# The first row tiles of a fused attention and FFN kernel: two PSUM tiles for the transposes, another load order, an earlier Sqrt table

## Chip, cores, metric

One core of a Trainium2 chip. The time is the device time of one execution in microseconds (us), median of several runs called fast (granted TensorE clock 0.998 to 1.000). The "span" is the time from the first to the last instruction of one profiled execution, about 1.8 us shorter than the device time of the same run.

Terms: a weight *piece* is one transfer; it has *landed* when the last of the 16 DMA engines that share it is through. A *PSUM tile* is a buffer for TensorE's results. A *hole* is a pause of TensorE between two matmuls. A *late run* is one that lies more than 0.5 us above the median of its kernel.

## The reference

`x` is (1, 2048, 640) in bf16. Cut to what matters:

```python
xn = (x - mean(x)) / sqrt(var(x) + 1e-5)            # per row of 640
s = attention(xn @ wq, k_cache[-512:], v_cache[-512:]) @ wo
g = silu((silu(xn @ w_gate) * (xn @ w_up)) @ w_down)  # hidden 1536
out = x + s * g
```

Everything starts with the normalisation and the FFN. This study is about the first 16 us of 924: the first rows of `x` and the first quarter of `w_gate` and `w_up` come in, four tiles of 128 rows are normalised, transposed on TensorE and multiplied by the first three hidden groups (f = 0 to 2, a gate and an up product each, so six PSUM banks). From group 3 on, matmuls of 512 columns run on all four row tiles at once.

## The kernel before

The loads. SyncE and ScalarE share them; the Sqrt table comes behind all of ScalarE's:

```python
load_x(0)                       # rows 0-63 on SyncE, 64-127 on ScalarE
load_x(1, nc.scalar)
for cs in (slice(0, 1), slice(1, 3), slice(3, NC)):     # NC = 5 chunks of 128 rows
    if cs.stop == NC:
        load_x(2)
    for eng, w_sb, w in ((nc.sync, wg_sb, B_w_gate), (nc.scalar, wu_sb, B_w_up)):
        ...                     # chunks cs, first 384 columns
load_x(3)
load_gu(1)                      # next quarter of both matrices
...
nc.scalar.activation(act_t[:], one_t[:], ACT.Sqrt)      # loads the table
keep_warm(11)                   # zero matmuls, 512 columns
```

The row tiles. All five transposes go into one PSUM tile, one or two copies take them out:

```python
def ready(t):
    ln_transpose(t)             # five TensorE transposes into tps[t], part of one tile tp
    n = NC if t else 2
    nc.scalar.copy(xnT[:, 0:n, rows], tps[t][:, 0:n, :])
    if n < NC:
        nc.vector.tensor_copy(out=xnT[:, n:NC, rows], in_=tps[t][:, n:NC, :])
...
ready(0); ln_sqrt(1); keep_warm(3)
for t in range(4):
    order = [(*fs, [c]) for c in range(NC) for fs in banks]      # chunk by chunk
    if t:
        order = [(*fs, range(NC)) for fs in banks]               # bank by bank
    for k, (f, s, cs) in enumerate(order):
        if k == len(order) * 3 // 5 and t < 3:
            ...                 # normalise tile t+1, ready(t + 1), statistics of the next
        hidden_mm(first[f][s][:, rows], s, f, rows, cs)
```

Then the loop over the hidden groups:

```python
for f in range(NF):
    if b or f >= 3:
        ffn_hidden(b, f)        # matmuls, Silu on ScalarE, product hT on VectorE
    if nx and 1 <= f < 5:
        ln_stats(4 * b + 3 + f) # statistics of the next block's row tiles, on VectorE
    if nx and 5 <= f < 9:
        ...                     # their normalisation and DMA transposes
```

The softmax here doesn't subtract the row's maximum and nothing guards it: scores larger than these inputs give would overflow.

Of the kernel before, what the change touches and what calls it, by code (L numbers as in the profile page):

```python
# [9 lines left out]
ACT = mybir.ActivationFunctionType  # L10
# [5 lines left out]
def kernel(  # L16
# [13 lines left out]
    nc = tc.nc  # L30
    P = nc.NUM_PARTITIONS

    x2 = A_x.flatten_outer_dims()
# [9 lines left out]
    NC = D // P  # L43
# [10 lines left out]
    bf = dt.bfloat16  # L54
    f32 = dt.float32
# [10 lines left out]
    wpool = ctx.enter_context(tc.tile_pool(name="att_w", bufs=2))  # L66
    kpool = ctx.enter_context(tc.tile_pool(name="att_k", bufs=1))
    qpool = ctx.enter_context(tc.tile_pool(name="att_q", bufs=2))
    psum = ctx.enter_context(tc.tile_pool(name="psum", bufs=2, space=bass.MemoryType.PSUM))

    def sc_tile():
        return psum.tile([P, 2, 512], f32, name="sc", tag="sc")

    def mm_tile():
        return psum.tile([P, 2, 512], f32, name="mm", tag="mm")


    ctx.enter_context(tc.manual_schedule())
# [1 line left out]
    xnT = res.tile([P, NC, Sq], bf, name="xnT")  # L80
# [3 lines left out]
    ident = consts.tile([P, P], bf, name="ident")  # L84
# [3 lines left out]
    one_t = consts.tile([P, 1], f32, name="one_t")  # L88
    nc.vector.memset(one_t[:], 1.0)
    act_t = consts.tile([P, 1], f32, name="act_t")  # L90
# [52 lines left out]
    def sum_k(pr, c):  # L143
        d = pairs[pr]
        nc.vector.reduce_sum(d["ssum"][:, c : c + 1], d["KT"][:, c, :], axis=AX.X)

    lo, hi = slice(0, 64), slice(64, 128)
# [17 lines left out]
    with ExitStack() as fctx:  # L165
# [6 lines left out]
        zero_t = ffw.tile([P, 512], bf, name="zero_t")  # L172
        nc.vector.memset(zero_t[:], 0.0)
        wg_sb = ffw.tile([P, NC, F], bf, name="wg_sb")
        wu_sb = ffw.tile([P, NC, F], bf, name="wu_sb")
        wd_sb = ffw.tile([P, NF, D], bf, name="wd_sb")
        FQ = F // 4
        x_t, ln, xns = {}, {}, {}

        def load_x(t, eng=nc.sync):  # L180
            x_t[t] = lnx.tile([P, D], bf, name="x_t")
            if t == 0:
                for r, eng in ((lo, nc.sync), (hi, nc.scalar)):
                    eng.dma_start(out=x_t[t][r, :], in_=x2[t * P + r.start : t * P + r.stop, :])
            else:
                eng.dma_start(out=x_t[t][:], in_=x2[t * P : (t + 1) * P, :])

        def load_gu(q):
            cols = slice(q * FQ, (q + 1) * FQ)
# [4 lines left out]
                out=wu_sb[:, :, cols], in_=B_w_up[:, cols].rearrange("(c p) f -> p c f", p=P)  # L194
            )

        load_x(0)
        load_x(1, nc.scalar)
        for cs in (slice(0, 1), slice(1, 3), slice(3, NC)):
            if cs.stop == NC:  # L200
                load_x(2)
            for eng, w_sb, w in ((nc.sync, wg_sb, B_w_gate), (nc.scalar, wu_sb, B_w_up)):
                src = w[cs.start * P : cs.stop * P, 0:FQ].rearrange("(c p) f -> p c f", p=P)
                eng.dma_start(out=w_sb[:, cs, 0:FQ], in_=src)
        load_x(3)
        load_gu(1)
        for t in range(4, 8):
# [3 lines left out]
        nc.sync.dma_start(out=wd_sb[:], in_=B_w_down.rearrange("(f p) d -> p f d", p=P))  # L211


        nc.scalar.activation(act_t[:], one_t[:], ACT.Sqrt)
        warm = sc_tile()

        def keep_warm(n):
            for _ in range(n):
                nc.tensor.matmul(warm[:, 0, :], zero_t[:, 0:P], zero_t[:], start=True, stop=True)

        keep_warm(11)

        def ln_stats(t, between=None):
            b, ti = divmod(t, 4)
            if ti == 0:
                ln[b] = [lnw.tile([P, 4, 2], f32, name="mv"), lnw.tile([P, 4], f32, name="rstd")]
            stats = lnw.tile([P, ng, nc.vector.BN_STATS_DIM], f32, name="stats")
            for g in range(ng):
                nc.vector.bn_stats(stats[:, g, :], x_t[t][:, g * (D // ng) : (g + 1) * (D // ng)])
                if g == 0 and between:  # L230
                    between()
            nc.vector.bn_aggr(ln[b][0][:, ti, :], stats[:])
# [7 lines left out]
        def ln_sqrt(t):  # L240
            mv, rstd = ln[0]
            nc.scalar.activation(
                rstd[:, t : t + 1], mv[:, t, 1:2], ACT.Sqrt, bias=eps_t[:], scale=1.0
            )
# [10 lines left out]
                    op0=ALU.subtract, op1=ALU.mult,  # L255
                )

        tps = {}

        def ln_transpose(t):  # L260
            xn = xns.pop(t)
            tps[t] = tp[:, t % 2, 0 : NC * P].rearrange("p (c k) -> p c k", c=NC)
            for c in range(NC):
                nc.tensor.transpose(tps[t][:, c, :], xn[:, c * P : (c + 1) * P], ident[:])

        def ln_transpose_dma(t):
            nc.sync.dma_start_transpose(
                out=xnT[:, 0:NC, t * P : (t + 1) * P], in_=xns.pop(t)[:]
            )
# [3 lines left out]
        def hidden_mm(out, s, f, qc, cs=range(NC)):  # L273
            w_sb = (wg_sb, wu_sb)[s]
            for c in cs:
                nc.tensor.matmul(  # L276
                    out, w_sb[:, c, f * P : (f + 1) * P], xnT[:, c, qc],
                    start=(c == 0), stop=(c == NC - 1),
                )

        def hidden_gate(b, f, g, u):
            sg = ffa.tile([P, 512], bf, name="sg")
            nc.scalar.activation(sg[:], g, ACT.Silu)  # L283
            nc.vector.tensor_tensor(hTs[b][:, f, :], u, sg[:], ALU.mult)  # L284

        def ffn_hidden(b, f):
            gu = mm_tile() if (b, f) == (0, 3) else sc_tile()
            for s in range(2):
                hidden_mm(gu[:, s, :], s, f, slice(b * 512, (b + 1) * 512))
            hidden_gate(b, f, gu[:, 0, :], gu[:, 1, :])  # L290

        def ffn_down(b, u):
            ti, n = divmod(u, 2)
# [23 lines left out]
        hTs[0] = ffh.tile([P, NF, 512], bf, name="hT")  # L317


        first = {f: [sc[:, s, :] for s in range(2)] for f, sc in ((0, sc_tile()), (1, sc_tile()))}  # L320
        tp = psum.tile([P, 2, 1024], bf, name="tp", tag="mm")
        first[2] = [mm[:, s, :] for mm in (mm_tile(),) for s in range(2)]
        def ready(t):
            ln_transpose(t)
            rows = slice(t * P, (t + 1) * P)
            n = NC if t else 2
            nc.scalar.copy(xnT[:, 0:n, rows], tps[t][:, 0:n, :])
            if n < NC:
                nc.vector.tensor_copy(out=xnT[:, n:NC, rows], in_=tps[t][:, n:NC, :])

        ln_stats(0)
        ln_sqrt(0)
        ln_stats(1, lambda: ln_apply(0, (slice(0, 2 * P), slice(2 * P, D))))
        ready(0)
        ln_sqrt(1)
        keep_warm(3)
        banks = [(f, s) for f in range(3) for s in range(2)]
        for t in range(4):
            rows = slice(t * P, (t + 1) * P)

            order = [(*fs, [c]) for c in range(NC) for fs in banks]
            if t:
                order = [(*fs, range(NC)) for fs in banks]
            for k, (f, s, cs) in enumerate(order):
                if k == len(order) * 3 // 5 and t < 3:
                    if t == 1:
                        ln_stats(3, lambda: ln_apply(2))
                    else:
                        ln_apply(t + 1)
                    ready(t + 1)  # L350
                    if t == 0:
                        ln_stats(2)
                    if t < 2:
                        ln_sqrt(t + 2)
                    else:
                        nc.scalar.activation(act_t[:], one_t[:], ACT.Silu)
                hidden_mm(first[f][s][:, rows], s, f, rows, cs)
                if t == 3 and s == 1:
                    hidden_gate(0, f, *first[f])
        nc.gpsimd.memset(V_p[:, :, :, Dh : Dh + 2], 1.0)  # L360

        for b in range(NB):
            if b:
                hTs[b] = ffh.tile([P, NF, 512], bf, name="hT")
            nx = b + 1 < NB
            u = 0
            for f in range(NF):
                if nx and b and f == 0:
                    for t in range(4 * b + 4, 4 * b + 8):
                        load_x(t)  # L370
                if b or f >= 3:
                    ffn_hidden(b, f)
                if nx and 1 <= f < 5:
                    ln_stats(4 * b + 3 + f)
                    if f == 4:
                        ln_rstd(b + 1, 0, 4)
                if nx and 5 <= f < 9:
                    ln_apply(4 * b + f - 1)
                    ln_transpose_dma(4 * b + f - 1)

                if b >= 1 and f % 3:
                    ffn_down(b - 1, u)
                    u += 1
                if b == 2:
                    if f == 0:
                        load_k(0)
                    elif 2 <= f < 6:
                        transpose_k(0, f - 2)
                    elif f == 6:
                        load_wq(0)  # L390
                    elif 7 <= f < 10:
                        sum_k(0, f - 7)
                elif b == 3:
                    if f < 5:
                        centre_k(0, f)
                    elif f < 8:
                        (load_k, load_wq, load_wo)[f - 5]((1, 1, 0)[f - 5])
# [360 lines left out]
```

## Time and profile before

| | before |
|---|---|
| device time, first three runs | 925.28 us (924.81 to 925.31) |
| span of the profiled run | 923.7 us |
| first real matmul | 6.91 us |
| first 512-column matmul (group 3) | 15.83 us |

TensorE sets the time, and after 15.83 us it waits for nothing that counts; so that start is the number to watch. The lines are shown in the prediction. A timeline line reads: start us, duration us, engine, source line, operation, `out<-in`, shapes, count; in brackets the idle time before it and what ended that. Several equal instructions in a row are merged, and matmuls overlap: one of 128 columns is shown 0.22 us long while the next starts 0.055 us after it. The distance of the starts is what a matmul costs.

### The profile page before, as it was taken

The page shows a single profiled execution, that of the slowest core. Times are in us where ns is not written, and L with a number is a line of the kernel's source. Part 1 is how long each engine was busy: PE and PEld are TensorE (multiplying, and loading weights), DVE is VectorE, ACT ScalarE, POOL GpSimd, SP SyncE. Part 2 cuts the span into 40 slices and gives each one's busy share as a digit, 9 for nine tenths or more (in the row PEclk, how much of TensorE's full clock was granted, in tenths as well). Part 3 has the DMA queues.
Part 4 walks back from the last instruction along what each step waited for, and adds up shares of the span by engine and source line. Part 5 has one row for each costly group of instructions (what it writes and reads, how often), then busy time and mean ns, then how long its engine had stood idle before and what let it go on. Part 6 is the DMA issues. An engine that isn't in the chain of part 4 may idle for free.

```text
span 923.7 us, 25785 instructions
## 1 busy us (share of the span) xinstructions
PE 917.0 (99%) x11101; PEld 626.2 (68%) x11101; DVE 576.2 (62%) x844; ACT 473.7 (51%) x847; POOL 100.1 (11%) x387
## 2 busy tenths in 40 slices
PE   9999999999999999999999999999999999999997
PEld 5455555575858585868686867676767777776665
DVE  6433331467676767676666667676767676767655
ACT  4222223546464656555556565655555555556561
POOL 0000000000000000000000000000000000002977
PEclk9999999999999999999999999999999999999999
DMA  9321510035544434444536252636271717162524
GB/s 294 77 53 35 114 35 1 1 71 95 83 82 83 83 79 87 74 91 68 98 59 106 60 107 53 112 51 115 44 121 41 126 37 129 36 132 74 135 57 140
DMA packets 243810, 77.18 MB, mean 84 GB/s; under 512 B 224624, under 2 KB 243696, under 8 KB 243696
## 3 DMA queue, kind: packets, MB, share of 16 engines
q1 hardware_dynamic: 242640, 74.72, 41.5%
q8 instruction: 87, 1.43, 0.7%
q10 hardware_dynamic: 1056, 0.82, 0.3%
q14 instruction: 27, 0.22, 0.1%
HBM read 39.45 MB, written 2.62 MB: 46 GB/s over the span
## 4 chain that ended last, share of the span: by engine, by line
PE 98%; DMA 1%; DVE 0%; ACTq 0%; issue 0%; DVEq 0%
PE mm L430 22%; PE sc L565 19%; PE sc L444 18%; PE mm L470 16%; PE sc L276 11%; PE mm L298 6%; PE sc L539 3%; PE mm L522 2%; PE mm L539 1%; DMA wu_sb<-in_B_w_up_dram 1%; PE mm L276 0%; PE mm L311 0%; PE sc L522 0%; PE sc L470 0%; PE mm L444 0%
## 5 line engine op out<-in xcount | busy, mean ns | idle before, releaser
L448 ACT ACTIVATE p_t<-sc 128x1024 bf16<-128x1024 f32 x254 | 252.9, 1022 | 128.6 <-PE sc L444 128.6
L435 DVE TENSOR_REDUCE qT<-mm 128x512 bf16<-128x1024 f32 x189 | 231.0, 1223 | 92.5 <-PE mm L430 90.0
L500 ACT ACTIVATE O_b<-mm,r 128x192 bf16<-128x192 f32 x486 | 164.6, 421 | 183.4 <-issue 159.2
L430 PE MATMUL mm<-xnT,wq_p 64*128 64x512 bf16 x1890 | 240.2, 377 | 0.0
L590 DVE TENSOR_TENSOR sacc<-sacc,sc 128x640 f32<-128x640 f32 x200 | 164.3, 821 | 89.5 <-PE sc L565 89.5
L565 PE MATMUL sc<-wo_p,OT_b 64*128 64x320 bf16 x2592 | 217.4, 296 | 0.0
L444 PE MATMUL sc<-qT,khat 64*128 64x512 bf16 x1524 | 198.4, 377 | 0.1
L470 PE MATMUL mm<-V_p,p_t 64*128 64x193 bf16 x3520 | 186.5, 243 | 0.0
L470 PEld LDWEIGHTS <-p_t 64*128 64x128 bf16 x3584 | 162.9, 93 | 12.3 <-issue 0.4
L430 PEld LDWEIGHTS <-wq_p 64*128 64x128 bf16 x1890 | 105.7, 94 | 94.5 <-issue 0.5
L565 PEld LDWEIGHTS <-OT_b 64*128 64x128 bf16 x2592 | 140.7, 94 | 21.1
L444 PEld LDWEIGHTS <-khat 64*128 64x128 bf16 x1536 | 85.9, 94 | 79.0 <-issue 0.4
L553 POOL MEMSET turn_t<- 128x1 f32 x328 | 32.2, 98 | 696.4 <-PE mm L470 474.0
L284 DVE TENSOR_TENSOR hT<-sc,sg 128x512 bf16<-128x512 f32 x46 | 31.7, 690 | 85.2 <-ACT sg L283 85.1
L283 ACT ACTIVATE sg<-sc 128x512 bf16<-128x512 f32 x46 | 27.3, 596 | 72.4 <-PE sc L276 72.4
L276 PE MATMUL sc<-xnT,wu_sb 128*128 128x512 bf16 (+1 forms) x260 | 59.1, 355 | 0.5 <-DMA wu_sb<-in_B_w_up_dram 0.5
L276 PE MATMUL sc<-xnT,wg_sb 128*128 128x512 bf16 (+1 forms) x260 | 59.2, 355 | 0.0
L298 PE MATMUL mm<-wd_sb,hT 128*128 128x320 bf16 x384 | 56.6, 300 | 0.0
L489 DVE RECIPROCAL r<-mm 128x4 f32<-128x4 f32 x124 | 22.6, 183 | 47.4 <-PE mm L470 35.9
L298 PEld LDWEIGHTS <-hT 128*128 128x128 bf16 x384 | 37.5, 98 | 18.9
L276 PEld LDWEIGHTS <-wu_sb 128*128 128x128 bf16 x285 | 26.3, 98 | 27.4 <-DMA wu_sb<-in_B_w_up_dram 0.7
L276 PEld LDWEIGHTS <-wg_sb 128*128 128x128 bf16 x285 | 26.4, 98 | 23.1
(68 smaller groups left out, 373.6 us busy)
## 6 DMA issues: line engine op xcount, KB each, us to landing
wo_p<-in_A_wo_dram SPq DMA_DIRECT2D x16, 480.0 KB, 4.3
K_p<-in_A_k_cache_dram SPq DMA_DIRECT2D x32, 192.0 KB, 3.1
V_p<-in_A_v_cache_dram SPq DMA_DIRECT2D x32, 192.0 KB, 3.0
wq_p<-in_A_wq_dram SPq DMA_DIRECT2D x64, 80.0 KB, 3.2
wq_p<-in_A_wq_dram SPq DMA_DIRECT2D x16, 160.0 KB, 3.5
x_r<-in_A_x_dram SPq DMA_DIRECT2D x16, 160.0 KB, 3.7
x_t<-in_A_x_dram SPq DMA_DIRECT2D x14, 160.0 KB, 3.1
OT_b<-O_b SPq DMA_TRANSPOSE x124, 2.8
```

Source lines behind the costliest of these rows:

```text
L276: nc.tensor.matmul(out, w_sb[:, c, f * P : (f + 1) * P], xnT[:, c, qc], start=(c == 0), stop=(c == NC - 1),)
L298: nc.tensor.matmul(dn[:, 0:HD], hTs[b][:, f, ti * P : (ti + 1) * P], wd_sb[:, f, cols], start=(f == 0), stop=(f == NF - 1),)
L430: nc.tensor.matmul(q_ps[:, h, :], pairs[pr]["wq"][r, c, j * P : (j + 1) * P], xnT[r, c, b * 512 : (b + 1) * 512], start=(c == 0), stop=(c ...
L435: nc.vector.reduce_sum(qTs[i][:, j, :], q_ps[:, :, :].rearrange("p h n -> p n h"), axis=AX.X)
L444: nc.tensor.matmul(sc[:, h, :], khat[r, j, ks], qT[r, j, :], start=(j == 0), stop=(j == 2))
L448: nc.scalar.activation(p_t[:, :, :], sc[:, :, :], ACT.Exp, scale=scale)
L470: m = nc.tensor.matmul(acc[:, k, h * 256 : h * 256 + Dh + 1], Ps[i][kc][r, h, qt * P : (qt + 1) * P], V_p[r, kc, h, 0 : Dh + 1], start=(p ...
L500: nc.scalar.activation(O_b[:, qt, h, :], a_k[:, h, 0:Dh], ACT.Copy, scale=r[:, k, h, :])
L539: nc.tensor.matmul(ps, OTs[i][:, 3 * qt + j, :], pairs[i // NB]["wo"][:, j, n * HD : (n + 1) * HD], start=(first and j == 0), stop=(end an ...
L553: st["turn"] = nc.gpsimd.memset(turn_t[:], 0.0)
L565: m = nc.tensor.matmul(ps[:, n, 0:HD], OTs[i][r, 3 * qt + j, :], pairs[i // NB]["wo"][r, j, n * HD : (n + 1) * HD], start=(turn == 0 and j ...
L590: nc.vector.tensor_tensor(s_t, s_t, sc[:, :, 0:HD], ALU.add)
```

## The change

Its intent: bring the first weights in earlier (one queue, four large pieces, x tiles 0 and 1 on the other queue), start the first matmuls after two transposes rather than five, and have the Sqrt table ready. The core of the diff:

```diff
-        load_x(0)
+        load_x(0, nc.scalar)
         load_x(1, nc.scalar)
-        for cs in (slice(0, 1), slice(1, 3), slice(3, NC)):
-            ...  (gate pieces on SyncE, up pieces on ScalarE, x tile 2 between)
+        load_first(slice(0, 2))          # gate and up, both on SyncE
+        load_first(slice(2, NC))
+        nc.scalar.activation(act_t[:], one_t[:], ACT.Sqrt)
+        load_x(2)
         load_x(3)
...
-        keep_warm(11)
+        keep_warm(9)
+        keep_warm(6, P)
...
         def ready(t):
-            ln_transpose(t)
-            ...
+            for tp, cs in zip(tps, PARTS):       # PARTS = chunks 0-1, chunks 2-4
+                for k, c in enumerate(range(cs.start, cs.stop)):
+                    nc.tensor.transpose(tp[:, k, :], xn[:, c * P : (c + 1) * P], ident[:])
+            ...  (one copy for each part; both on ScalarE, the second on VectorE for t == 3)
-        keep_warm(3)
...
-            if t:
+            if t == 3:
                 order = [(*fs, range(NC)) for fs in banks]
-                if k == len(order) * 3 // 5 and t < 3:
+                if k == len(order) * 4 // 5 and t < 3:
...
+        ffn_hidden(0, 3, [...])                  # group 3, in the banks of the two transpose tiles
+        early.close()                            # then the early PSUM pool gives way to "mm"
...
-                if b or f >= 3:
+                if b or f >= 4:
                     ffn_hidden(b, f)
```

Group 3 has to leave the loop, as it uses the early PSUM pool.

More of the change, by code (lines that the diff above doesn't have):

```diff
@@ L68 @@
     qpool = ctx.enter_context(tc.tile_pool(name="att_q", bufs=2))
-    psum = ctx.enter_context(tc.tile_pool(name="psum", bufs=2, space=bass.MemoryType.PSUM))
+    sc_pool = ctx.enter_context(tc.tile_pool(name="psum_sc", bufs=2, space=bass.MemoryType.PSUM))
+    mm_pool = []
     def sc_tile():
-        return psum.tile([P, 2, 512], f32, name="sc", tag="sc")
+        return sc_pool.tile([P, 2, 512], f32, name="sc")
     def mm_tile():
-        return psum.tile([P, 2, 512], f32, name="mm", tag="mm")
+        return mm_pool[0].tile([P, 2, 512], f32, name="mm")
     ctx.enter_context(tc.manual_schedule())
@@ L181, in load_x, with load_first @@
             x_t[t] = lnx.tile([P, D], bf, name="x_t")
-            if t == 0:
-                for r, eng in ((lo, nc.sync), (hi, nc.scalar)):
-                    eng.dma_start(out=x_t[t][r, :], in_=x2[t * P + r.start : t * P + r.stop, :])
-            else:
-                eng.dma_start(out=x_t[t][:], in_=x2[t * P : (t + 1) * P, :])
+            eng.dma_start(out=x_t[t][:], in_=x2[t * P : (t + 1) * P, :])
+        def load_first(cs):
+            for w_sb, w in ((wg_sb, B_w_gate), (wu_sb, B_w_up)):
+                src = w[cs.start * P : cs.stop * P, 0:FQ].rearrange("(c p) f -> p c f", p=P)
+                nc.sync.dma_start(out=w_sb[:, cs, 0:FQ], in_=src)
         def load_gu(q):
@@ L195, in load_gu @@
             )
-        load_x(0)
+        load_x(0, nc.scalar)
         load_x(1, nc.scalar)
-        for cs in (slice(0, 1), slice(1, 3), slice(3, NC)):
-            if cs.stop == NC:
-                load_x(2)
-            for eng, w_sb, w in ((nc.sync, wg_sb, B_w_gate), (nc.scalar, wu_sb, B_w_up)):
-                src = w[cs.start * P : cs.stop * P, 0:FQ].rearrange("(c p) f -> p c f", p=P)
-                eng.dma_start(out=w_sb[:, cs, 0:FQ], in_=src)
+        load_first(slice(0, 2))
+        load_first(slice(2, NC))
+        nc.scalar.activation(act_t[:], one_t[:], ACT.Sqrt)
+        load_x(2)
         load_x(3)
@@ L211, with keep_warm @@
         nc.sync.dma_start(out=wd_sb[:], in_=B_w_down.rearrange("(f p) d -> p f d", p=P))
-        nc.scalar.activation(act_t[:], one_t[:], ACT.Sqrt)
-        warm = sc_tile()
-        def keep_warm(n):
-            for _ in range(n):
-                nc.tensor.matmul(warm[:, 0, :], zero_t[:, 0:P], zero_t[:], start=True, stop=True)
-        keep_warm(11)
+        early = ExitStack()
+        psum1 = early.enter_context(tc.tile_pool(name="psum1", bufs=1, space=bass.MemoryType.PSUM))
+        PARTS = (slice(0, 2), slice(2, NC))
+        tps = [psum1.tile([P, 8, P], bf, name="tp", tag="tp%d" % n) for n in range(2)]
+        first = [
+            [gu[:, s, :] for s in range(2)]
+            for gu in (sc_tile(), sc_tile(), psum1.tile([P, 2, 512], f32, name="gu"))
+        ]
+        def keep_warm(n, cols=512):
+            for _ in range(n):
+                nc.tensor.matmul(
+                    first[2][1][:, 0:cols], zero_t[:, 0:P], zero_t[:, 0:cols], start=True, stop=True
+                )
+        keep_warm(9)
+        keep_warm(6, P)
         def ln_stats(t, between=None):
@@ L256, in ln_apply @@
                 )
-        tps = {}
-        def ln_transpose(t):
-            xn = xns.pop(t)
-            tps[t] = tp[:, t % 2, 0 : NC * P].rearrange("p (c k) -> p c k", c=NC)
-            for c in range(NC):
-                nc.tensor.transpose(tps[t][:, c, :], xn[:, c * P : (c + 1) * P], ident[:])
         def ln_transpose_dma(t):
@@ L284, in hidden_gate, with ffn_hidden @@
             nc.vector.tensor_tensor(hTs[b][:, f, :], u, sg[:], ALU.mult)
-        def ffn_hidden(b, f):
-            gu = mm_tile() if (b, f) == (0, 3) else sc_tile()
+        def ffn_hidden(b, f, gu=None):
+            gu = gu or [sc[:, s, :] for sc in (sc_tile(),) for s in range(2)]
             for s in range(2):
-                hidden_mm(gu[:, s, :], s, f, slice(b * 512, (b + 1) * 512))
-            hidden_gate(b, f, gu[:, 0, :], gu[:, 1, :])
+                hidden_mm(gu[s], s, f, slice(b * 512, (b + 1) * 512))
+            hidden_gate(b, f, *gu)
         def ffn_down(b, u):
@@ L317 @@
         hTs[0] = ffh.tile([P, NF, 512], bf, name="hT")
-        first = {f: [sc[:, s, :] for s in range(2)] for f, sc in ((0, sc_tile()), (1, sc_tile()))}
-        tp = psum.tile([P, 2, 1024], bf, name="tp", tag="mm")
-        first[2] = [mm[:, s, :] for mm in (mm_tile(),) for s in range(2)]
         def ready(t):
-            ln_transpose(t)
-            rows = slice(t * P, (t + 1) * P)
-            n = NC if t else 2
-            nc.scalar.copy(xnT[:, 0:n, rows], tps[t][:, 0:n, :])
-            if n < NC:
-                nc.vector.tensor_copy(out=xnT[:, n:NC, rows], in_=tps[t][:, n:NC, :])
+            xn, rows = xns.pop(t), slice(t * P, (t + 1) * P)
+            for tp, cs in zip(tps, PARTS):
+                for k, c in enumerate(range(cs.start, cs.stop)):
+                    nc.tensor.transpose(tp[:, k, :], xn[:, c * P : (c + 1) * P], ident[:])
+            for tp, cs in zip(tps, PARTS):
+                part = tp[:, 0 : cs.stop - cs.start, :]
+                if t == 3 and cs.stop == NC:
+                    nc.vector.tensor_copy(out=xnT[:, cs, rows], in_=part)
+                else:
+                    nc.scalar.copy(xnT[:, cs, rows], part)
         ln_stats(0)
@@ L359 @@
                     hidden_gate(0, f, *first[f])
+        ffn_hidden(0, 3, [psum1.tile([P, 512], f32, name="gu3", tag="tp%d" % n)[:, :] for n in range(2)])
+        early.close()
+        mm_pool.append(ctx.enter_context(tc.tile_pool(name="psum_mm", bufs=2, space=bass.MemoryType.PSUM)))
         nc.gpsimd.memset(V_p[:, :, :, Dh : Dh + 2], 1.0)
```

## The prediction

> **What bounds the kernel now.** I read the cores view first (one core, 923.7 us, clock 1.000), then the page's head: TensorE is busy for nearly the whole span, and the chain that ended last is TensorE for 98% of it.
>
> ```profile
> PE 917.0 (99%) x11101; PEld 626.2 (68%) x11101; DVE 576.2 (62%) x844; ACT 473.7 (51%) x847; POOL 100.1 (11%) x387
> ...
> PE 98%; DMA 1%; DVE 0%; ACTq 0%; issue 0%; DVEq 0%
> ```
>
> So the time is TensorE's work plus what TensorE loses, and the waits view of TensorE says where it loses: from 16 us to the end one wait of 0.2 us, before 16 us these two.
>
> ```profile
> PE sc L219 <- DVE zero_t L173: 1.2, 1, 1.2
> PE sc L276 <- DMA wu_sb<-in_B_w_up_dram: 0.5, 1, 0.5
> ```
>
> The change touches only the first 16 us, so I read these closely. First the chain of waits for the first 20 us (start us, us, what): it leaves TensorE at 8.09 us for a weight transfer that ScalarE's queue issued at 2.42 us and that took 5.62 us.
>
> ```profile
> 1.94 0.45 ACTq L204
> 2.39 0.03 issue
> 2.42 5.62 DMA wu_sb<-in_B_w_up_dram
> 8.04 0.05 issue
> 8.09 0.34 PE sc L276 x3
> ```
>
> Then the timeline, all engines (start us, us, engine, line, operation; in brackets the idle time before and what ended it). It has the path from x tile 0 to the first real matmul, and the stall.
>
> ```profile
> 1.23 4.79 PE L219 MATMUL sc<-zero_t 128*128 128x512 bf16 x11 [1.23 <-DVE zero_t L173]
> 3.48 1.28 ACT L214 ACT_TABLE_LOAD   x1 [3.48 <-DMA x_t<-in_A_x_dram]
> 3.65 0.89 DVE L229 BATCH_NORM_STATS2 stats<-x_t 128x6 f32<-128x320 bf16 x2 [2.48 <-DMA x_t<-in_A_x_dram]
> 4.88 0.28 ACT L242 ACTIVATE rstd<-mv,eps_t 128x1 f32<-128x1 f32 x1
> 5.39 0.64 DVE L253 TENSOR_SCALAR xn<-x_t,mv,rstd 128x256 bf16<-128x256 bf16 x2
> 5.86 0.57 PE L264 MATMUL tp<-ident,xn 128*128 128x128 bf16 x5
> 6.46 0.37 ACT L327 COPY xnT<-tp 128x256 bf16<-128x256 bf16 x1 [1.30 <-PE tp L264]
> 6.86 0.36 DVE L329 COPY xnT<-tp 128x384 bf16<-128x384 bf16 x1 [0.19 <-ACT xnT L327]
> ```
>
> TensorE's own timeline shows the first matmul at 6.91 us, the seventh at 7.35, the eighth at 8.09, and the first 512-column one (hidden group f=3) at 15.83. From there on nothing holds TensorE, so 15.83 us is the number to move.
>
> ```profile
> 6.91 0.22 PE L276 MATMUL sc<-xnT,wg_sb 128*128 128x128 bf16 x1
> ...
> 7.35 0.22 PE L276 MATMUL sc<-xnT,wg_sb 128*128 128x128 bf16 x1
> 8.09 0.23 PE L276 MATMUL sc<-xnT,wu_sb 128*128 128x128 bf16 x1 [0.52 <-DMA wu_sb<-in_B_w_up_dram]
> ...
> 15.83 1.03 PE L276 MATMUL mm<-xnT,wg_sb 128*128 128x512 bf16 x4
> ```
>
> Between 8.09 and 15.83 us stand 113 matmuls and 15 transposes, all of 128 columns, whose starts lie 0.0555 us apart: 128 x 0.0555 = 7.10 us. The other 0.64 us are small holes: 0.1 us before 9.09, and 0.04 to 0.15 us at each later row tile, while one ScalarE copy of 640 columns (0.69 us) is waited for.
>
> **What the Trainium skill says.** (1) "DMA: Bandwidth & Descriptors", section "Queues, rings and completion order": the queues of SyncE and ScalarE are rings on the same 16 engines, which take turns between them; descriptors of one ring start in order. The trace agrees: the weight piece issued at 2.42 us landed at 8.04 us, when 1.58 MB had moved, though the pieces issued up to and with it are 896 KB (0.92 MB). The other 0.66 MB came later (x tiles 2 and 3, chunks 3 and 4, the next quarter) and went past it. (2) "TensorE: Matmul & The Clock Gate", section "The HAM clock gate": a cold array runs at half rate until a free-running window of about 3.4 us was busy. The trace agrees: warm-up matmuls start 0.427 us apart until 5.47 us, those after 6.26 us 0.216 us apart. (3) "ScalarE: Activation LUTs", section "What ACT_TABLE_LOAD costs": about 1283 ns. Here 1.28 us.
>
> **The change part by part.**
>
> *Loads.* ScalarE issues x tiles 0 and 1 only; SyncE issues four weight pieces (chunks 0-1 of both matrices, 192 KB each; chunks 2-4, 288 KB each), then x tiles 2 and 3. With one queue for the weights nothing issued later can pass them. The DMA view of before gives 0.19 MB moved by 3 us, 0.52 by 4, 0.72 by 5, 0.97 by 6, 1.29 by 7 and 1.58 by 8; the last packet of x tile 0 and its landing lie 0.41 us apart. At that pace: chunks 0-1 with both x tiles (704 KB, 0.72 MB) at 5.0 + 0.4 = 5.4 us; gate chunks 2-4 (1.02 MB) at 6.1 + 0.4 = 6.5; up chunks 2-4 (1.31 MB) at 7.1 + 0.4 = 7.5; x tile 2 at 7.9, x tile 3 at 8.5. Two corrections: of the 16 engines' shares of the piece landing at 8.04 us the first was in at 5.47 us and most by 6.3, so the slowest engine may add half a microsecond or more; and the thin stretch from 4.0 to 4.5 us (146 GB/s against 259 in the two microseconds before), when half the engines had nothing, should fill, which takes some 0.2 us off. My choice for up chunks 2-4: 7.8 us, between 7.0 and 8.6.
>
> *x tile 0.* One queue instead of two halves, beside weights rather than alone: 8 packets of each engine now alternate with weight packets. Before, ScalarE's half landed at 3.04 and SyncE's at 3.52. I take 3.55 to 3.8, a cost of 0 to 0.2 us.
>
> *Sqrt table.* It starts near 1.95 us rather than 3.48 and is done by 3.25. Before, the variance was ready at 4.78 us and the square root started at 4.88, so the table cost 0.1 us at most. It pays for the later x tile.
>
> *Two transpose tiles.* Before, the ScalarE copy waited for all five transposes (6.43 us). Now it needs two, done near 6.05: copy of 256 columns from 6.1 to 6.5, first matmul near 6.55 instead of 6.91. The second copy (384 columns; 0.69 us for 640 and 0.37 for 256 give 0.48) runs from 6.45 to 6.95 on ScalarE; chunk 2 is wanted after 12 matmuls, 6.55 + 0.67 = 7.2. The copy is hidden, the weights are not: up chunk 2 is there at 7.8. TensorE stops after 13 matmuls rather than 7 and resumes at 7.8 rather than 8.09.
>
> *Chunk-first order and transposes at 4/5.* For tiles 0 to 2 six matmuls (0.33 us) and three transposes (0.17 us) now stand behind the first part's copy, which takes 0.37 us and a handshake: the holes should close. Normalisation must keep up: tile 1 normalised at 7.8 us as before; tile 2, whose statistics start near 8.3 us, at about 10.4; tile 3 at about 12. TensorE wants them after 24 matmuls of the tile before: near 8.5, 10.5 and 12.4. Just in time, with 0.1 us lost perhaps.
>
> *Sum.* Left at 7.8 us: 17 + 90 matmuls and 15 transposes = 122 x 0.0555 = 6.77, plus 0.15 of holes: f=3 starts at 14.7 us, against 15.83. Gain 1.1 us, all on the path, as TensorE never waits after that. No arithmetic is removed but the three warm-up matmuls at 6.26 to 6.91 us, which filled a wait. 925.3 - 1.1 = 924.2; I take 924.1, as the early stage has one more small chance each way.
>
> **Rivals.** (a) *The weights arrive in time* (up chunks 2-4 by 7.2 us). For it: all weights are issued by about 3 us and queued in order. Against: packets of up to 0.8 us between 4 and 7.5 us. Then only TensorE counts: 6.55 + 135 x 0.0555 = 14.05, with 0.3 of holes 14.35: gain 1.5, 923.8. (b) *The stall only moves* to chunk 2 and ends at 8.6 us or later, the slowest engine deciding: f=3 at 15.5, gain 0.3, 925.0. For it: that same set of bytes was in at 9.05 us before, with x tile 2 and some of 3 ahead of the last piece. (c) *The clock stays cold.* Warm-up now ends near 5.7 us instead of 5.96, and three filler matmuls are gone. If full speed came 2 us later, some 18 matmuls at 0.107 us cost 1 us, and the gain is gone: 925.2. Against: the clock of before rose at about 5.8 us, with the same work ahead of it. (d) *x tiles 2 and 3 come later*, behind all first weights, and tile 2's transposes wait: gain 0.5 us smaller.
>
> **Range and chances.** Between rivals (a) and (b) lie 923.8 and 925.0; the three runs of before spread by 0.5 us, so 8 in 10 for 923.0 to 925.2. Two per cent would be 18.5 us, over the whole first stage: 0.01 faster, 0.98 within, 0.01 slower.
>
> **What would show it.** First real matmul near 6.55 us and the first copy before the fifth transpose ends; the stall, if any, after 13 matmuls, at chunk 2, released by the up-weight transfer; the Sqrt table load near 2 us; first 512-column matmul between 14.3 and 15.5 us; the rest of the trace shifted unchanged. Wrong if x tile 0 lands after 4.0 us, if the transposes or early matmuls start 0.107 us apart after 6.3 us, or if TensorE waits for DVE at tiles 2 and 3 by more than 0.3 us.

## The result and the profile after

| | before | after |
|---|---|---|
| device time, median of 6 runs | 925.18 us (924.81 to 925.66) | 924.28 us (924.18 to 925.76) |
| the same, second session | 925.30 us (9 runs) | 924.45 us (5 runs) |
| span of the profiled run | 923.7 us | 922.4 us |
| first real matmul | 6.91 us | 6.50 us |
| last first-quarter weight piece landed | 9.05 us | 7.26 us |
| first 512-column matmul | 15.83 us | 14.53 us |
| from there to the first down projection | 23.74 us | 24.02 us |

A ratio of times is the mean of one kernel's fast runs over that of the other's in the same rounds, so not quite the ratio of the medians: here 0.9993, 95% interval 0.998 to 1.0005. That interval contains 1: the gain of 0.9 us is a thousandth, and by this measure it is not settled. For a gain speaks that 9 of the 11 runs of the changed kernel lie under the fastest of the 15 runs of before (924.57 or less, against 924.81), and that the traces show where the time went. The page of the changed kernel:

```profile
PE 914.8 (99%) x11086; PEld 625.3 (68%) x11102; DVE 576.4 (62%) x844; ACT 474.0 (51%) x850; POOL 100.1 (11%) x387
...
PE 98%; DVE 1%; DMA 0%; issue 0%; ACT 0%; DVEq 0%
```

The bound is still TensorE; a new 1% of the chain runs through VectorE. The waits of TensorE over the whole span name no weight transfer any more:

```profile
PE gu L225 <- DVE zero_t L174: 1.2, 1, 1.2
PE tp L326 <- DVE xn L262: 0.7, 1, 0.7
```

The timeline, all engines, up to the first copy. The table load starts at 1.66 us instead of 3.48; x tile 0 is there at 3.65 as before; the copy starts at 6.07 us, before the fifth transpose ends, instead of 6.46:

```profile
1.66 1.28 ACT L203 ACT_TABLE_LOAD   x1 [1.66 <-PEq L747]
...
3.65 0.89 DVE L238 BATCH_NORM_STATS2 stats<-x_t 128x6 f32<-128x320 bf16 x2 [2.48 <-DMA x_t<-in_A_x_dram]
...
4.82 0.29 ACT L251 ACTIVATE rstd<-mv,eps_t 128x1 f32<-128x1 f32 x1 [1.67 <-DVE mv L241]
...
5.75 0.63 PE L326 MATMUL tp<-ident,xn 128*128 128x128 bf16 x5 [0.70 <-DVE xn L262]
...
6.07 0.82 ACT L332 COPY xnT<-tp 128x256 bf16<-128x256 bf16 x2 [0.96 <-PE tp L326]
```

TensorE's timeline: 13 matmuls from 6.50 us on, then a hole of 0.09 us (7.16 to 7.31) for the up chunks that landed at 7.26; later a hole of 0.12 us for the first copy at each of the next three tiles (the last at 12.64); the first 512-column matmul at 14.53.

```profile
6.50 0.22 PE L277 MATMUL sc<-xnT,wg_sb 128*128 128x128 bf16 x1
...
7.16 0.22 PE L277 MATMUL sc<-xnT,wg_sb 128*128 128x128 bf16 x1
7.31 0.23 PE L277 MATMUL sc<-xnT,wu_sb 128*128 128x128 bf16 x1
...
14.53 1.24 PE L277 MATMUL gu<-xnT,wg_sb 128*128 128x512 bf16 x4
```

Why the weights came earlier shows in the table by stretches (stretch, its length, busy us of PE, PEld, DVE, ACT, POOL, then clock, DMA share, GB/s). Before:

```profile
4.00:4.50 0.50, 0.50 (x2) 0.15 (x1) 0.50 (x2) 0.50 (x1) 0.00 (x0) 1.00 0.59 146
4.50:6.00 1.50, 1.50 (x6) 0.47 (x4) 1.37 (x7) 0.65 (x3) 0.00 (x0) 1.00 0.89 253
```

After:

```profile
4.00:4.50 0.50, 0.50 (x3) 0.20 (x2) 0.50 (x2) 0.00 (x0) 0.00 (x0) 1.00 1.07 360
4.50:6.00 1.50, 0.80 (x10) 0.43 (x7) 1.43 (x7) 0.29 (x1) 0.00 (x0) 1.00 1.05 330
```

So the transfers did not only come in another order; between 4 and 6 us they also ran at 330 to 360 GB/s instead of 146 to 253.

And the 0.28 us lost after group 3? VectorE's timeline before: the statistics of x tiles 4 and 5, the product of group 3 (19.97), the statistics of tile 6, the product of group 4 (21.56), without a pause.

```profile
17.94 0.88 DVE L229 BATCH_NORM_STATS2 stats<-x_t 128x6 f32<-128x320 bf16 x2
...
18.98 0.83 DVE L229 BATCH_NORM_STATS2 stats<-x_t 128x6 f32<-128x320 bf16 x2
...
19.97 0.64 DVE L284 TENSOR_TENSOR hT<-mm,sg 128x512 bf16<-128x512 f32 x1
20.52 0.88 DVE L229 BATCH_NORM_STATS2 stats<-x_t 128x6 f32<-128x320 bf16 x2
...
21.56 0.64 DVE L284 TENSOR_TENSOR hT<-sc,sg 128x512 bf16<-128x512 f32 x1
```

After: group 3 was called ahead of the loop, so its product comes first, and all three tiles of statistics stand behind it:

```profile
16.97 0.69 DVE L285 TENSOR_TENSOR hT<-gu,sg 128x512 bf16<-128x512 f32 x1 [0.28 <-PE gu L277]
17.57 0.88 DVE L238 BATCH_NORM_STATS2 stats<-x_t 128x6 f32<-128x320 bf16 x2
...
18.61 0.83 DVE L238 BATCH_NORM_STATS2 stats<-x_t 128x6 f32<-128x320 bf16 x2
...
19.61 0.83 DVE L238 BATCH_NORM_STATS2 stats<-x_t 128x6 f32<-128x320 bf16 x2
...
20.60 0.64 DVE L285 TENSOR_TENSOR hT<-sc,sg 128x512 bf16<-128x512 f32 x1
```

The work ahead of the product of group 4 is the same in both: three tiles of statistics and the product of group 3. What is new is the idle time in brackets: VectorE waits 0.28 us for TensorE to finish group 3, where before it did statistics. Counted from the start of group 3, the product of group 4 ends at 6.37 us before and at 6.71 us after. TensorE needs the PSUM tile of group 4 for group 6. Before, it got there at 6.47 us (22.30), just behind that product; after, the product ends at 21.24 us, and group 6 starts at 21.29, 1.36 us after the five matmuls before it, where five take 1.08:

```profile
19.93 1.24 PE L277 MATMUL sc<-xnT,wu_sb 128*128 128x512 bf16 x5
21.29 1.24 PE L277 MATMUL sc<-xnT,wg_sb 128*128 128x512 bf16 x5
```

Sum of the two profiled runs: -1.30 us up to group 3, +0.28 up to the first down projection, 0.00 to 0.02 in all that follows up to the last matmul of the output projection, -0.25 in the last five microseconds: -1.27, from 923.72 to 922.45. Whether the last term belongs to the change is not shown: from the start of the last matmul to the end it is 5.00 and 4.99 us in the two traces with the load order of before, and 4.67 to 4.86 in the eleven others. The run of before that was profiled was a slow one of its kind (its span 923.7, the median of nine others 923.5), so 0.9 and not 1.3 us is the typical gain.

### The profile page after: what moved, and what is told of

Its sections match the earlier page's. It is cut to its first block, busy times and chain, and to the rows that moved or that the text cites. A ratio compares the mean times of both kernels' runs of the same rounds, so it can differ in the third digit from the quotient of the medians.

```text
span 922.4 us, 25771 instructions
## 1 busy us (share of the span) xinstructions
PE 914.8 (99%) x11086; PEld 625.3 (68%) x11102; DVE 576.4 (62%) x844; ACT 474.0 (51%) x850; POOL 100.1 (11%) x387
## 4 chain that ended last, share of the span: by engine, by line
PE 98%; DVE 1%; DMA 0%; issue 0%; ACT 0%; DVEq 0%
PE mm L435 22%; PE sc L570 19%; PE sc L449 18%; PE mm L475 16%; PE sc L277 10%; PE mm L299 6%; PE sc L544 3%; PE mm L527 2%; PE mm L544 1%; PE gu L277 0%; DVE stats L238 0%; PE mm L312 0%; DMA x_t<-in_A_x_dram 0%; PE sc L527 0%; PE sc L475 0%
```

## The experiments

All kernels gave correct results. The first four ran on one chip with nine runs of before, the next four on another, each with nine runs of before of its own; a difference "to before" is that of medians.

### The changed kernel again

> The changed kernel once more, to see how far its runs spread and whether the moment at which TensorE goes to full speed moves with them. In the first profiles full speed began at 5.8 us before the change and at 4.0 us after it. Theory (the early stage decides): the first 512-column matmul again at 14.4 to 14.7 us, span 922.4, median 924.2 to 924.4, about 1.0 under the kernel before. Rival (the start of full speed decides): a run whose full speed begins later than 6.5 us shows early matmuls 0.107 us apart, a 512-column start up to 1 us later, and a time near 925.5, like the one run of 925.76.

Measured: median 924.45 us (924.30, 924.30, 924.45, 924.57, 925.45), before 925.30. The profile: full clock at 4.1 us, the last up piece landed at 7.52 us, and TensorE waited 0.35 us for it; group 3 at 14.79 us, then 24.02 us to the first down projection. So the early stage decides again, and its end follows the landing of that piece. The late run, 925.45, was not the profiled one.

### Only the loads

```diff
 (kernel before)
-        load_x(0) ... the three gate/up pieces on two queues ...
+        load_x(0, nc.scalar); load_x(1, nc.scalar)
+        load_first(slice(0, 2)); load_first(slice(2, NC))
+        nc.scalar.activation(act_t[:], one_t[:], ACT.Sqrt)
+        load_x(2)
```

> Only the load order and the place of the Sqrt table are changed; transposes, copies, matmul order and warm-up are those of before. Theory (the weight transfer was the bound and one queue in order removed it): first matmul still near 6.9 us, last first-quarter weight piece landed by 7.4 us, no wait of TensorE for weights, first 512-column matmul near 15.0 us (6.9 + 135 x 0.0555 + 0.6 of holes), so 0.8 us of the 1.3 us. Rival (the two transpose tiles and the chunk-first order carry the gain): 15.5 us or later, under 0.4 us gained.

Measured: median 924.83 us, 0.47 under before; three runs at 924.52 to 924.83, two at 925.50 and 925.56. The profile fell on a late one, and the expectation of "no wait for weights" failed in it. The waits of TensorE:

```profile
PE sc L274 <- DMA wu_sb<-in_B_w_up_dram: 0.7, 1, 0.7
```

The up piece of chunks 2 to 4 landed at 8.43 us, although half of the sixteen engines had their share in by 6.50 and fifteen by 6.87. One engine was 1.6 us behind, and group 3 started at 16.10 us, later than before. By medians the loads alone carry about half of the gain (0.47 of 0.85 us), in the good runs most of it (the best is 0.8 us under before); one late engine takes it back. The Sqrt table moved together with the loads here and was never tested alone.

### Only the transposes, copies and order

The changed kernel with the load order and the Sqrt place of before.

> The two transpose tiles, chunk-first order, the later transposes and the shorter warm-up, with the load order of before. Theory: the first matmul is near 6.5 us but TensorE then stops for the same weights as before, at about 8.1 us, and again for chunks 3 and 4 near 9; first 512-column matmul 15.6 to 15.9 us, gain 0 to 0.2 us. Rival (these parts carry the gain): 14.5 to 15.0 us, gain 0.8 us or more.

Measured: median 925.81 us (925.70 to 926.11), 0.51 above before. First matmul at 6.61 us; then a stop for up chunks 1-2 until 7.93 and one for gate chunks 3-4 until 8.93; group 3 at 15.87 us, as expected. Beyond expectation it is slower: 24.01 us instead of 23.74 from group 3 on, the same 0.28 as in the full change. So this part alone brings nothing up to group 3, as the weights stop TensorE anyway, and costs 0.28 us later. The remaining 0.2 us lie within the spread of the runs of before. The two halves don't add up (0.47 gained and 0.51 lost alone, 0.85 gained together): the transposes pay only once the weights are there. On top of the loads they bring 0.38 us by medians, although the 0.28 us are lost.

### The up pieces on ScalarE's queue

```diff
-                nc.sync.dma_start(out=w_sb[:, cs, 0:FQ], in_=src)
+                (nc.sync if w_sb is wg_sb else nc.scalar).dma_start(out=w_sb[:, cs, 0:FQ], in_=src)
```

> The changed kernel with its same four large weight pieces, but the two of the up matrix issued on the queue of ScalarE behind the x tiles. Theory (what helps is that on one queue in order nothing later passes the weights): the last up piece lands about 0.8 us later than the 7.26 us of the changed kernel, near 8.1; TensorE stops for it after 13 matmuls; first 512-column matmul near 15.3 us, most of the gain gone. Rival (the larger pieces or the free ScalarE are what helps): 14.5 to 14.7 us as in the changed kernel.

Measured: median 924.92 us, 0.47 above the changed kernel. The profile fell on the slowest run (925.52), so what it shows is more than the typical loss. The last up piece landed at 8.29 us (half of its engines at 7.49, against 6.57 to 6.62 in the two profiles of the changed kernel), TensorE stopped 0.95 us after 13 matmuls, group 3 at 15.55. The pieces were the same size; the queue made the difference. The theory holds in kind: x tiles 2 and 3, issued on the other queue, landed ahead of the last up piece (6.55 and 7.91 us). In this late run the expected 15.3 was 0.25 short, part of it a full clock that came only at 6.81 us.

### Two x tiles ahead of the second weight pieces

```diff
         load_first(slice(0, 2))
+        load_x(2); load_x(3)
         load_first(slice(2, NC))
```

> The changed kernel with x tiles 2 and 3 (320 KB) on the queue of SyncE ahead of the second pair of weight pieces instead of behind them. Theory (one queue is served in order, so what stands ahead delays what stands behind by its bytes): the last up piece lands 0.9 us later (328 KB at some 350 GB/s), typically near 8.2 us, TensorE stops for it after 13 matmuls, first 512-column matmul 15.3 to 15.6 us, median 0.6 to 0.9 us above the changed kernel. Rival (the order does not matter, only that ScalarE issues no weights): 14.5 to 14.8 us.

Measured: median 924.92 us, 0.5 to 0.6 above the changed kernel of the other calls. Half of the engines had the last up piece at 7.50 us, 0.9 us later, as the bytes say; the slowest had it at 7.83, as it was not far behind this time, so TensorE stopped 0.33 us instead of 0.9. Group 3 at 15.09 us, under the expected 15.3 to 15.6. Order on one queue matters by its bytes; the slowest engine adds its own amount. With two queues half of the engines had the piece at 7.49 us, the same as here: it fits that what the second queue cost were the same two x tiles going ahead.

### No warm-up matmuls

```diff
-        keep_warm(9)
-        keep_warm(6, P)
```

> The changed kernel without its 15 warm-up matmuls. If the start of full speed matters as much as the prediction's third rival said, the first real matmuls start 0.107 us apart from 6.5 us until TensorE has been busy[...], near 10 to 13 us: 30 to 60 matmuls lose 0.05 us each, first 512-column matmul 16 to 17.5 us, median 1.5 to 3 us above the changed kernel. If it does not matter (the stage is bound by the weights and by VectorE's normalisation): within 0.5 us of the changed kernel.

Measured: median 925.80 us, 1.35 to 1.5 above the changed kernel, just under the range. TensorE's timeline around the change of clock, at 9.6 us in the trace: starts 0.107 us apart before, 0.055 after.

```profile
9.04 0.31 PE L275 MATMUL gu<-xnT,wg_sb 128*128 128x128 bf16 x1
9.15 0.31 PE L275 MATMUL gu<-xnT,wu_sb 128*128 128x128 bf16 x1
...
9.71 0.22 PE L275 MATMUL sc<-xnT,wg_sb 128*128 128x128 bf16 x1
9.76 0.22 PE L275 MATMUL sc<-xnT,wu_sb 128*128 128x128 bf16 x1
```

So the clock counts in this stage, and the warm-up is worth 1.4 us. With it, full speed began between 4.04 and 7.11 us in twelve traces, and the latest (7.11, in the run with x tiles ahead) cost 0.22 us on five matmuls. That is too little for the late runs near 925.5, which lie 1 us and more above the others.

### The gate matmuls of chunks 2 to 4 first

```diff
+            if t == 0:
+                order = order[:12] + [(f, s, [c]) for s in range(2) for c in range(2, NC) for f in range(3)]
```

> The changed kernel with, in row tile 0, all nine gate matmuls of chunks 2 to 4 ahead of the nine of up, so that the last up piece is wanted after 21 matmuls, near 7.67 us, instead of after 13, near 7.22. In four traces with the new load order this piece landed at 7.26, 7.52, 8.29 and 8.43 us, always by its slowest DMA engine, while half the engines had it by 6.6. Theory (the runs near 925.5 are those whose slowest engine is late): no hole where it lands by 7.65; the late runs lose 0.45 us less; median 0.1 to 0.3 us under the changed kernel, highest run under 925.2. Rival (late runs come from something else, such as the start of full speed): spread and median unchanged.

Measured: median 924.34 us (924.09 to 924.43, no late run), 0.88 under before, as the changed kernel. In the profiled run the piece landed at 7.01 us, so it shows no hole but would not have had one anyway. Inconclusive here; more below. (The 8.29 us in the expectation are the run with two queues, where half of the engines had the piece at 7.49 us and not by 6.6.)

### The statistics one group later

```diff
-                if nx and 1 <= f < 5:
-                    ln_stats(4 * b + 3 + f)
+                g = f - (b == 0)
+                if nx and 1 <= g < 5:
+                    ln_stats(4 * b + 3 + g)
 (and the same for the normalisation and transposes)
```

> The changed kernel with the statistics of x tiles 4 to 7 and their normalisation asked for one hidden group later in the first block, so that VectorE does the product of group 4 before the third of them. In the traces with the change TensorE starts group 6 only 6.76 us after group 3, without it 6.47; from group 3 to the first down projection 24.02 against 23.74. Theory (the pulled-forward group 3 put three tiles of statistics ahead of the product of group 4, whose PSUM tile group 6 needs): 23.74 us again, median 0.28 us under the changed kernel, near 924.1. Rival (the other PSUM layout or the banks of group 3 make the hole): 24.02 us remain.

Measured: median 924.16 us, but 24.03 us from group 3 to the first down projection remained. (The words "put three tiles of statistics ahead" are not quite right: three stood there before too, see above.) By its number the rival won; the trace says otherwise. Group 6 started at 20.94 us, 6.47 after group 3: that hole was gone. A new one of the same size stood at the first group of the next block, as my edit had moved the last normalised tile and its DMA transpose (which that group reads) one group later too:

```profile
32.81 1.24 PE L277 MATMUL sc<-xnT,wu_sb 128*128 128x512 bf16 x5
34.18 1.02 PE L277 MATMUL sc<-xnT,wg_sb 128*128 128x512 bf16 x4
```

### One swap on VectorE

```diff
-                    ln_stats(4 * b + 3 + f)
+                    for t in ((), (4,), (5,), (6, 7))[f - 1] if b == 0 else (4 * b + 3 + f,):
+                        ln_stats(t)
```

> The changed kernel with one swap on VectorE: the statistics of x tile 6 behind the product of group 4 instead of ahead of it; tiles 4, 5 and 7, the normalisation and the transposes stay where they were. The run that moved everything one group later filled the hole before group 6 (group 3 to group 6 in 6.47 us) but TensorE then stopped 0.29 us at the first group of the next block, for the last transposed tile. Theory: no hole at either place, 23.74 us from group 3 to the first down projection, median 924.0. Rival (the product of group 4 is not what group 6 waits for): a hole of 0.28 us remains at one of the two places and the median stays at 924.2 to 924.4.

Measured: 23.74 us from group 3 to the first down projection, no hole. VectorE still waits 0.28 us for group 3, but the product of group 4 now has two tiles of statistics ahead of it. Median 924.04 us (923.91, 923.92, 924.04, 924.72, 925.10), 1.15 under before. This settles where the 0.28 us went: the order of calls on VectorE, not the PSUM layout.

The profile fell on the latest run (925.10) and shows what a late run is. The DMA view of the first 3 us (size of each, us from issue to landing) has these weight pieces of chunks 2 to 4:

```profile
wg_sb<-in_B_w_gate_dram SPq DMA_DIRECT2D x1, 288.0 KB, 5.8
wu_sb<-in_B_w_up_dram SPq DMA_DIRECT2D x1, 288.0 KB, 6.2
```

In the changed kernel's first profile the DMA view has 4.6 and 5.0 us for the same two.

The up piece landed at 8.43 us, with half of its engines in by 6.53 and fifteen by 7.54; TensorE stopped 0.55 us for gate and 0.84 for up, and group 3 began at 15.69 us. Full speed began at 4.56 us, early: the clock is not the cause.

### Swap and gates first together

> The same, and the gate matmuls of chunks 2 to 4 ahead of those of up in row tile 0. Theory (the late runs are late because of the slowest engine's part of the last up piece): group 3 starts at 14.4 to 14.6 us, 23.74 us after it, span near 922.0, median 923.8 to 924.1, no run above 924.8. Rival (late runs have another cause): one in five or six runs still lies 1 us above the others.

Measured: median 924.00 us (923.89, 923.89, 924.00, 924.28, 925.13), 1.19 under before; 23.74 us after group 3, which began at 14.65 (full speed at 6.87 us, 0.1 us lost by it). One late run remained, against the theory's "none above 924.8". It was not profiled. With gates first 1 of 15 runs was later than 924.6 (this one); in the changed kernel and the two with its matmul order and shifted statistics 4 of 21. That is too few to tell. The edit can hide 0.45 us at most, and an engine that is late with the gate piece as well is not helped by it, as the swap run's 0.55 us at gate shows.

### The transposes after 22 matmuls

```diff
-                if k == len(order) * 4 // 5 and t < 3:
+                if k == len(order) * 3 // 4 and t < 3:
```

> The same, with the transposes of the next row tile after 22 of 30 matmuls instead of 24. Behind each of tiles 1 to 3 TensorE waits 0.12 us for the first copy. Theory of the small holes (two more matmuls, 0.11 us, cover the copy): the three holes go, group 3 starts near 14.1 us, 0.3 us earlier. Rival (VectorE's normalisation, ready only 0.13 to 0.16 us before the transposes, becomes the bound): the holes move to the transposes and group 3 starts at 14.3 to 14.4 us, at most 0.1 us gained.

Measured: median 923.77 us (923.72 to 924.19), before 925.19: 1.42 under it, ratio 0.9986, interval 0.9974 to 0.9999. The best kernel. Group 3 at 14.37 us. The three holes behind the transposes went, and holes of 0.11, 0.08 and 0.03 us came ahead of them: the rival was right, VectorE's normalisation is the next bound. Part of the 0.23 us to the run before is luck with the clock (5.38 us here, 6.87 there).

## Why the prediction was right or wrong

The time, 924.28 us against a predicted 924.1, was in the range. That it came so close is luck in part: the last up piece was 0.5 us earlier than foretold, holes of 0.26 us more and the 0.28 us after group 3 took that back. The steps behind it:

- **x tile 0, table, first matmul.** Right: landed at 3.63 us (3.55 to 3.8 foretold; before, SyncE's half landed at 3.55, not at 3.52); the square root at 4.82 instead of 4.88 us; the copy at 6.07, the first matmul at 6.50 (6.55).
- **The stall moves to up chunk 2, after 13 matmuls.** Right as to its place: the matmul at 7.31 us is the fourteenth, and in the second profile it waited 0.35 us there.
- **"Up chunks 2-4: 7.8 us, between 7.0 and 8.6."** Mis-sized. In nine traces with the weights in order on one queue alone, seven have it at 6.93 to 7.52 us and two at 8.43. The common case is near rival (a)'s 7.2, the two late ones come near rival (b)'s 8.6, and 7.8 was hit by none. I had taken the pace of the DMA from before and 0.2 us off; by 7 us before had moved 1.29 MB and the changed kernel 1.63. The reading of 0.66 MB that "went past" the piece of before was too strong: when the last up piece of the changed kernel landed, 1.73 MB had moved, 0.42 more than the pieces up to and with it, although they stood in order on their queue. So much of that lead can come from engines that are through before the slowest one; only x tile 2 (issued later, landed at 7.84 us) is seen to pass as a whole. Here the Trainium skill, "DMA: Bandwidth & Descriptors", section "Queues, rings and completion order", fits: on one ring the order of issue kept, and the run with up pieces back on the second ring lost 0.47 us.
- **"The holes should close", 0.15 us in all.** Mis-sized. Three holes of 0.12 us stayed, behind the first copy of each tile; with a small one they make 0.41 us in the changed kernel, apart from the weight wait. Two matmuls more behind the transposes closed them and opened others ahead of them.
- **"All on the path, as TensorE never waits after that" and "the rest of the trace shifted unchanged".** Wrong, and it is the step that failed in kind. The change took group 3 out of the loop; my list of its parts left that out. VectorE, which takes its calls in order, then waited 0.28 us for group 3 with all the statistics behind it; the product that frees the PSUM tile for group 6 came later, and 0.28 us of the gain was given back. The swap of two calls returned them. That the order on VectorE sets it is shown by that swap; that the wait for group 3 is what was new is read from the two traces, and no run takes that wait away alone.
- **Rival (c), the clock.** Less than a quarter of its foretold 1 us at the worst seen: 0.22 us for full speed at 7.11 us, 1.3 us later than before and not 2. Without any warm-up it costs 1.4 us.
- **Rival (d), late x tiles.** Did not come: x tiles 2 and 3 landed at 7.72 and 8.17 us in the changed kernel.

Typical gain: about 1.2 us up to group 3 (1.30 and 1.04 in the two profiles) less 0.28, which is the measured 0.85 to 0.9. What stays open is the cause of the late runs, 7 of the 45 runs with the weights in order on one queue alone. Two of the seven were profiled, and both show one or two of the sixteen DMA engines 0.9 to 1.8 us behind the others; for the other five that is not shown. No instruction fetch lies in the trace between the start and 14 us. In the late swap run no single packet between 2.5 and 9 us took over 0.25 us; in the run with only the loads five between 4.8 and 6.1 us took 0.29 to 0.60, which would be enough if all were one engine's, but the profile does not say whose they were.

## What to carry to other kernels

A load that gates the start belongs on one queue in the order of need, with nothing that is needed later on a second queue beside it; judge it by its slowest engine, not by the mean. When a call leaves a loop, look at what it overtakes on every engine in order: a call that comes before its data is there makes the engine wait, with everything behind it, and a product that frees a PSUM buffer should not stand behind work that nobody waits for. And a gain read off one stage must be followed to the next two buffer reuses before it is booked.

## What the Trainium skill lacked or had wrong

- "TensorE: Matmul & The Clock Gate", section "The HAM clock gate": it gives the moment of full speed as about 4 us into the matmuls, varying by 500 ns either way from run to run; its note that one kernel had 6, 11 or 14 slow matmuls allows more. Here, with the warm-up starting at 1.23 us every time, it came between 4.04 and 7.11 us in twelve traces, 2.8 to 5.9 us after that start; without warm-up it came 3.7 us after the first transpose.
- "ScalarE: Activation LUTs", section "What ACT_TABLE_LOAD costs": it adds a drain of about 1380 ns to the 1283 ns of the load. The load of 1.28 us is confirmed; no such drain is seen, neither behind the load (1.66 to 2.94 us, the next activation at 2.95) nor ahead of it (the load of the Silu table starts at 12.78 us, 0.02 us after the end of the copy before it).
- "DMA: Bandwidth & Descriptors", section "Rules for kernel authors": spreading DMAs over several issuing engines for bandwidth "Doesn't help"; it lacks that it can hurt. Here it did: 924.92 us with the up pieces on the second queue, 924.45 with all on one.
- The same page, section "Why a DMA increments its semaphore by 16 and not by 1", says that the up to sixteen engines of a transfer finish independently, but no page has a size for it. For the last up piece in nine traces: half of them were through at 6.5 to 6.7 us, the last at 6.93 to 7.52 in seven and at 8.43 in two.
